# Tiny products taken away ahead of six 448-token slots, and six long warming products instead of eleven short ones

## The chip, the cores and the metric

The kernel runs on one core of one Trainium2 chip. A core has five engines with queues of their own: TensorE (PE: its products are PE, its weight loads PEld, and they overlap), VectorE (DVE), ScalarE (ACT), GpSimd (POOL) and SyncE (SP, which here issues DMAs). The metric is the device time of one execution in microseconds (us). A profile of one execution shows the span from its first to its last instruction; the execution's own time is a little longer than its span.

## The reference

Attention with a sigmoid in place of a softmax, then a mixture of experts that sends each token to one expert:

```
attention   q, k, v: (8, 12, 448, 64)
  attn = sigmoid(q k^T / 8 - log 448);  x = attn v, as (3584 tokens, 768)
experts     w1: (8, 768, 1024), w2: (8, 1024, 768)
  e(token)  = argmax(x @ w_gate);  p = its softmax probability
  g(token)  = sigmoid(x @ w_output_gate)[e]
  out       = p * g * (relu(x @ w1[e]) @ w2[e])
```

All is float32. How many tokens each expert gets is known only at run time.

## The kernel before

**Attention.** TensorE computes scores and values of all heads, 64 columns of weights at a time (lines 720 and 729). Between the stages of a batch the gate products (line 781) and the routing put each token's row into the list of its expert.

**Warming.** At the very start TensorE has no data. `attention` lets it multiply eleven times a constant column that is broadcast to 256 columns (line 811), before the first scores (line 720), which wait for the first DMAs of q and k.

**Experts, in slots.** The tokens of an expert are worked off in slots of 448 tokens, and what is left over in slots of 240 at the end. A 448-token slot does layer 1 (eight blocks f, six inner steps d each) and layer 2 (six blocks c, eight inner steps f each). Numbers are split into a high and a low part, so that each inner step is three products. In the first slot they have 448 columns each (lines 471 to 473 and 512 to 514). In every later 448-token slot the method `products` does a step with 512, 384 and 448 columns (lines 483, 484 and 485), so that layer 1 is 48 such triples and layer 2 another 48. With the inputs here seven 448-token slots run: the first from `build` with its first block begun inside the attention, three more in straight code after it (second to fourth in all), and the fifth, sixth and seventh each in a block that is entered under a condition (`tc.If`, line 936). Two 240-token slots end the kernel.

**Order of the work.** It is written out by hand (`manual_schedule`): in every block of layer 1 and layer 2 the gathers of the next slot's tokens (POOL, line 390), its weight loads (SP), and the splits of weights and tokens (ACT line 415, DVE line 416) stand between the products, so that the next slot's operands are ready when its first block comes.

**Tiny products.** `slots_begun` counts the 448-token slots that are finished. In `layer1_mm`, ahead of the first block (f == 0) of a 448-token slot, TensorE multiplies a zero tile (bfloat16) by a few of its own columns, into the PSUM bank that the block's first real product then overwrites:

```
KICKS = ((), (), (8,), (8, 8, 8), (64,), (64, 64), (128,))        # line 51
for cols in KICKS[self.slots_begun] if ... else ():               # line 465
    nc.tensor.matmul(ps[:, 0:cols], self.zero, self.zero[:, 0:cols], start=True, stop=True)
```

So there are none ahead of the first and the second slot, one of 8 columns ahead of the third, three of 8 ahead of the fourth, one of 64, two of 64 and one of 128 ahead of the fifth, sixth and seventh. Two further tiny products of the same kind (`change_step`, line 457) stand in the first slot, after its first block.

Of the kernel before, what the change touches and what calls it, by code (L numbers as in the profile page):

```python
# [30 lines left out]
TB = 448  # L31
# [16 lines left out]
ROUNDED = (12 * DF + 12 * TB) * 4  # L48
XG = GB_ * Q4 * 4
PLAIN = 6 * DF * 4 + XG + 6 * TB * 4  # L50
KICKS = ((), (), (8,), (8, 8, 8), (64,), (64, 64), (128,))


def r32(ap):
    return ap.bitcast(F32)


class Kernel:
# [400 lines left out]
    def layer1_mm(self, f, n):  # L459
        nc = self.nc  # L460
        ps = self.h_ps = self.take("h", self.psh)
        c = slice(128 * f, 128 * f + 128)
        (wh, wl), (xh, xl) = self.w1s, self.xs
        if f == 0 and n == TB:
            for cols in KICKS[self.slots_begun] if self.slots_begun < len(KICKS) else ():
                nc.tensor.matmul(ps[:, 0:cols], self.zero, self.zero[:, 0:cols], start=True, stop=True)
        for d in range(6):
            if n == TB and self.joined:
                mm = self.products(ps, wh[d][:, c], wl[d][:, c], self.x2[:, d], d == 0, d == 5)
            else:  # L470
                nc.tensor.matmul(ps[:, 0:n], wh[d][:, c], xh[:, d, 0:n], start=(d == 0), stop=False)  # L471
                nc.tensor.matmul(ps[:, 0:n], wh[d][:, c], xl[:, d, 0:n], start=False, stop=False)  # L472
                mm = nc.tensor.matmul(ps[:, 0:n], wl[d][:, c], xh[:, d, 0:n], start=False, stop=(d == 5))  # L473
            if d == 2:
                self.beat[1] = mm.ins
# [201 lines left out]
    def attention(self, pool):  # L677
        nc = self.nc
# [28 lines left out]
        def load_v(g):  # L707
            b, hp = divmod(G * g, NPAIR)
            v = vv[g % 3]
            nc.sync.dma_start(v[:, :, 0:3], self.vm[b, hp:hp + G].rearrange("g p c j d -> p g c j d"))  # L710
            for i in range(G):
                nc.sync.dma_start(v[half[i], i, 3], self.ve[b, hp + i])
# [76 lines left out]
                    want[0] = next(routes[0])  # L789

        nc.vector.memset(r32(self.rounded[:, 0:8]), 0.0)
        warm = self.rounded[:, 0:1].broadcast_to([128, 256])
        nc.vector.memset(self.bias_s, -math.log(S))
        def load_first():
            first, rest = slice(0, 128), slice(128, S)
# [11 lines left out]
        for g in (1, 2):  # L807
            load_qk(g)
            load_v(g)
        for _ in range(11):  # L810
            nc.tensor.matmul(self.ps_o[1][0][:, 0:256], warm[:, 0:128], warm, start=True, stop=True)
        LAG = 2
        for u in range(U * NG + LAG):
            g, i = divmod(u, U)
# [175 lines left out]
```

## Time and profile before

| | |
|---|---|
| time, median of 3 runs | 755.86 us (755.49 to 756.57) |
| the profiled execution's own time | 756.47 us |
| its span | 754.6 us |
| mean granted TensorE clock | 0.998 of full speed |
| PE busy | 745.1 us (99%), 5589 products |
| PEld busy | 572.3 us (76%) |
| DVE, ACT, POOL busy | 447.9, 370.4, 251.5 us (59%, 49%, 33%) |

A product's shown duration reaches past the start of the next one, since products are pipelined. What a product costs TensorE is the distance from its start to the next start.

### The profile page before, as it was taken

To read this page: it belongs to the slowest core of one execution; us is meant where nothing else is said; L and a number is where in the kernel's file an instruction comes from. 1 tells how busy PE (TensorE), PEld (TensorE's weight loads), DVE (VectorE), ACT (ScalarE), POOL (GpSimd) and SP (SyncE) were. 2 spreads that over 40 slices of the span, in tenths; PEclk is the share of its full clock that TensorE was granted. 3 is DMA by queue.
4 is the path that set the end of the run, shared out by engine and by line. 5 is a ranking of instruction groups with operands and counts; after the bars stand their busy time and mean duration, and the time that the engine had idled before them with its cause. 6 is when DMAs were issued, how large, how long until landed. Compare 5 with 4: busy or idle time off the path is not lost. (4 is left out here: it accounts for less than half of the span.)

```text
span 754.6 us, 14707 instructions
## 1 busy us (share of the span) xinstructions
PE 745.1 (99%) x5589; PEld 572.3 (76%) x5589; DVE 447.9 (59%) x895; ACT 370.4 (49%) x437; POOL 251.5 (33%) x375
## 2 busy tenths in 40 slices
PE   9999999999999999999999999999999999999996
PEld 6666444444465479999988888889989998889996
DVE  1343853586687759825836826836645665566555
ACT  6665666576776733414523514504514433444644
POOL 5000130031444436147335225315325234233461
PEclk9999999999999999999999999999999999999999
DMA  9464665746695646457387376376385476567851
GB/s 310 138 187 154 189 148 172 216 120 183 229 317 181 166 135 214 122 148 229 124 272 252 114 237 214 137 234 218 123 276 176 171 261 182 185 226 241 282 198 46
DMA packets 90647, 145.76 MB, mean 193 GB/s; under 512 B 16738, under 2 KB 67298, under 8 KB 90560
## 3 DMA queue, kind: packets, MB, share of 16 engines
q1 hardware_dynamic: 79808, 119.22, 51.1%
q0 software_dynamic: 9680, 24.53, 9.3%
q10 hardware_dynamic: 1072, 0.92, 0.5%
q8 instruction: 46, 0.75, 0.4%
q14 instruction: 41, 0.34, 0.1%
HBM read 118.40 MB, written 32.62 MB: 200 GB/s over the span
## 5 line engine op out<-in xcount | busy, mean ns | idle before, releaser
L722 ACT ACTIVATE a<-ps,small 128x896 f32<-128x896 f32 x168 | 168.9, 1007 | 84.8 <-PE ps L720 83.3
L720 PE MATMUL ps<-q,k 64*64 64x448 f32 x1344 | 179.2, 539 | 0.3
L729 PE MATMUL ps<-a,v 64*64 64x448 f32 x1344 | 178.6, 536 | 0.0
L390 POOL DMA_INDIRECT plain<-x_dram,lxs x112 | 111.0, 991 | 142.5 <-ACT h L500 66.2
L500 ACT ACTIVATE h<-ps 128x448 fp32r<-128x448 f32 (+1 forms) x72 | 36.4, 506 | 214.5 <-DVE ps L490 161.8
L729 PEld LDWEIGHTS ps<-a,v 64*64 64x64 f32 x1344 | 66.9, 133 | 62.8 <-issue 43.8
L720 PEld LDWEIGHTS ps<-q,k 64*64 64x64 f32 x1344 | 66.3, 134 | 62.8 <-issue 43.3
L483 PE MATMUL ps<-rounded 128*128 128x512 f32 x288 | 113.5, 394 | 0.0
L483 PE MATMUL ps<-h,w2h 128*128 128x512 f32 x288 | 113.1, 393 | 0.0
L485 PE MATMUL ps<-h,w2l 128*128 128x448 f32 x288 | 106.1, 368 | 0.0
L485 PE MATMUL ps<-rounded 128*128 128x448 f32 x288 | 106.0, 368 | 0.0
L416 DVE TENSOR_TENSOR rounded<-plain,rounded 128x2048 fp32r<-128x2048 f32 (+5 forms) x63 | 96.5, 1566 | 10.6 <-ACT rounded L415 10.5
L484 PE MATMUL ps<-rounded 128*128 128x384 f32 x288 | 96.8, 336 | 1.1 <-issue 1.1
L484 PE MATMUL ps<-h,w2h 128*128 128x384 f32 x288 | 96.7, 336 | 0.0
L415 ACT CAST rounded<-plain 128x2048 fp32r<-128x2048 f32 (+5 forms) x63 | 82.0, 1333 | 24.3 <-DVE plain L435 23.1
L489 DVE COPY hb<-ps 128x64 f32<-128x64 f32 x84 | 18.5, 221 | 101.2 <-PE ps L485 83.8
L575 POOL DMA_INDIRECT out<-y,lts x24 | 42.8, 1785 | 106.8 <-ACT y L568 105.0
L501 DVE SCALAR_TENSOR_TENSOR h<-ps,h 128x448 fp32r<-128x448 f32 (+1 forms) x72 | 41.3, 574 | 44.4 <-ACT h L500 37.2
L416 DVE TENSOR_TENSOR w2l<-plain,w2h 128x768 fp32r<-128x768 f32 x72 | 65.8, 954 | 3.1 <-ACT w2h L415 0.7
L485 PEld LDWEIGHTS ps<-h,w2l 128*128 128x128 f32 x288 | 54.0, 187 | 12.4
L485 PEld LDWEIGHTS ps<-rounded 128*128 128x128 f32 x288 | 54.0, 187 | 12.3
L484 PEld LDWEIGHTS ps<-rounded 128*128 128x128 f32 x288 | 54.1, 188 | 6.5 <-issue 1.5
(172 smaller groups left out, 1016.2 us busy)
## 6 DMA issues: line engine op xcount, KB each, us to landing
plain<-w SPq DMA_DIRECT2D x40, 768.0 KB
plain<-w SPq DMA_DIRECT2D x27, 1024.0 KB
k<-kT SPq DMA_DIRECT2D x23, 448.0 KB
q<-qT SPq DMA_DIRECT2D x23, 448.0 KB
x_dram<-xt SPq DMA_DIRECT2D x30, 336.0 KB
v<-vm SPq DMA_DIRECT2D x23, 384.0 KB
y<-y_dram SPq DMA_DIRECT2D x18, 384.0 KB
y_dram<-plain SPq DMA_DIRECT2D x28, 192.0 KB
```

Source lines behind the costliest of these rows:

```text
L390: self.paced(self.nc.gpsimd.indirect_dma_start(out=self.xg[:, g], out_offset=None, in_=x4, in_offset=bass.IndirectOffsetOnAxis(ap=s["lx"][ ...
L415: self.nc.scalar.copy(hi, raw)
L416: self.nc.vector.tensor_tensor(lo, raw, r32(hi), ALU.subtract)
L483: mm(ps, wh, both[:, 0:512], start=first, stop=False)
L484: mm(ps[:, 512 - TB:TB], wh, both[:, 512:2 * TB], start=False, stop=False)
L485: return mm(ps[:, 0:TB], wl, both[:, 0:TB], start=False, stop=last)
L500: self.beat[0] = nc.scalar.activation(hh, ps, AF.Relu).ins
L501: nc.vector.scalar_tensor_tensor(hl, ps, 0.0, r32(hh), ALU.max, ALU.subtract)
L575: i = self.nc.gpsimd.indirect_dma_start(out=self.out, out_offset=bass.IndirectOffsetOnAxis(ap=at, axis=0), in_=y, in_offset=None, bounds_c ...
L720: qk = nc.tensor.matmul(ps[half[h], j, 0:S], k[half[j], e, o:o + 64], q[half[j], e], start=True, stop=True)
L722: self.beat[0] = nc.scalar.activation(at[u % 3], ps[:, :, 0:S], AF.Sigmoid, bias=self.bias_s, scale=1.0 / math.sqrt(D)).ins
L729: nc.tensor.matmul(self.ps_o[e][h][half[j], 0:S], v[half[h], e, c, j], a[half[h], j], start=(i in ((0, 3 if h else 4)[e],)), stop=(i == (2 ...
```

## The change

Two edits. The table of tiny products and the loop that issues them go: no tiny product stands ahead of any 448-token slot any more (those of `change_step` in the first slot stay). And the warming products at the start are six of 512 columns instead of eleven of 256, into the same PSUM bank.

```
-KICKS = ((), (), (8,), (8, 8, 8), (64,), (64, 64), (128,))
...
     def layer1_mm(self, f, n):
...
-        if f == 0 and n == TB:
-            for cols in KICKS[self.slots_begun] if self.slots_begun < len(KICKS) else ():
-                nc.tensor.matmul(ps[:, 0:cols], self.zero, self.zero[:, 0:cols], start=True, stop=True)
         for d in range(6):
...
-        warm = self.rounded[:, 0:1].broadcast_to([128, 256])
+        warm = self.rounded[:, 0:1].broadcast_to([128, 512])
...
-        for _ in range(11):
-            nc.tensor.matmul(self.ps_o[1][0][:, 0:256], warm[:, 0:128], warm, start=True, stop=True)
+        for _ in range(6):
+            nc.tensor.matmul(self.ps_o[1][0], warm[:, 0:128], warm, start=True, stop=True)
```

## Rows read from the trace of the kernel before

**Rows 1.** The page: the span, and busy time, share and products of PE.
```profile
span 754.6 us, 14707 instructions
PE 745.1 (99%) x5589; PEld 572.3 (76%) x5589; DVE 447.9 (59%) x895; ACT 370.4 (49%) x437; POOL 251.5 (33%) x375
```

**Rows 2.** Waits of PE: line, waited for, us in total, times, longest.
```profile
PE ps L484 <- issue: 1.1, 1, 1.1
...
PE ps L471 <- DVE hb L489: 0.6, 1, 0.6
```

**Rows 3.** Windows, line 483 alone, slots two to seven: window, its us, busy (products).
```profile
329.39:385.79 56.40, 36.59 (x94) 17.46 (x93) 1.00 0.62 193
386.53:445.43 58.90, 37.65 (x95) 17.68 (x94) 1.00 0.64 213
446.21:505.10 58.89, 37.64 (x95) 17.70 (x94) 1.00 0.61 201
505.83:562.84 57.01, 36.98 (x95) 17.65 (x94) 1.00 0.64 206
566.17:621.98 55.81, 36.20 (x93) 17.27 (x92) 1.00 0.61 200
622.71:680.99 58.28, 37.25 (x95) 17.69 (x94) 1.00 0.63 205
```

**Rows 4.** Line 483, second slot: ns min/median/max, first and last start.
```profile
L483 PE MATMUL ps<-h,w2h x48: 389/389/390, 357.0 to 385.2; 128*128 128x512 f32 x48
L483 PE MATMUL ps<-rounded x46: 388/389/390, 329.4 to 356.4; 128*128 128x512 f32 x46
```

**Rows 5.** The same of the third slot.
```profile
L483 PE MATMUL ps<-h,w2h x48: 395/396/397, 415.7 to 444.8; 128*128 128x512 f32 x48
L483 PE MATMUL ps<-rounded x47: 395/396/397, 386.5 to 415.1; 128*128 128x512 f32 x47
```

**Rows 6.** Timeline of PE, second slot into third: start us, us, line.
```profile
385.58 0.37 PE L485 MATMUL ps<-h,w2l 128*128 128x448 f32 x1
385.79 0.18 PE L466 MATMUL ps<-zero 128*128 128x8 bf16 x1
385.83 0.48 PE L483 MATMUL ps<-rounded 128*128 128x512 f32 x1
...
386.53 0.40 PE L483 MATMUL ps<-rounded 128*128 128x512 f32 x1
```

**Rows 7.** Timeline of PEld there.
```profile
385.42 0.19 PEld L485 LDWEIGHTS ps<-h,w2l 128*128 128x128 f32 x1
385.79 0.10 PEld L466 LDWEIGHTS <-zero 128*128 128x128 bf16 x1 [0.18 <-issue]
```

**Rows 8.** Timeline of PE, first slot into second.
```profile
328.15 0.39 PE L483 MATMUL ps<-rounded 128*128 128x512 f32 x1
...
328.78 0.40 PE L483 MATMUL ps<-rounded 128*128 128x512 f32 x1
```

**Rows 9.** Timeline of PE, early in the sixth slot.
```profile
563.60 0.40 PE L483 MATMUL ps<-rounded 128*128 128x512 f32 x1
565.08 0.45 PE L484 MATMUL ps<-rounded 128*128 128x384 f32 x1 [1.08 <-issue]
```

**Rows 10.** Windows, all engines, fourth and fifth slot: us, busy of PE, PEld, DVE, ACT, POOL.
```profile
446.21:505.10 58.89, 58.89 (x286) 52.19 (x285) 34.55 (x59) 21.96 (x26) 20.71 (x18) 1.00 0.61 201
505.83:562.84 57.01, 57.01 (x286) 51.74 (x285) 34.32 (x59) 21.97 (x26) 20.73 (x18) 1.00 0.64 206
```

**Rows 11.** Lines 811 and 720, the start: ns min/median/max, first and last start.
```profile
L811 PE MATMUL ps<-rounded x11: 420/421/582, 0.9 to 3.2; 128*128 128x256 f32 x11
L720 PE MATMUL ps<-q,k x4: 975/1002/1003, 3.8 to 3.8; 64*64 64x448 f32 x4
L720 PE MATMUL ps<-q,k x20: 536/537/611, 4.5 to 6.2; 64*64 64x448 f32 x20
```

**Rows 12.** Timeline of PEld at the first scores.
```profile
3.75 0.33 PEld L720 LDWEIGHTS ps<-q,k 64*64 64x64 f32 x8 [0.39 <-DMA q<-qT]
```

## The prediction

> **What bounds the kernel now.** I read the page first: PE is busy 99% of the span and no other engine over 76% [rows 1]. Next the waits of PE, to see whether a data wait hides in that: after the start there are two, 1.1 us put down to issue and 0.6 us for DVE ahead of the first 240-token slot [rows 2]. So the time of the experts is the time that TensorE takes from one product to the next, and whatever shortens that distance shortens the kernel.
>
> Then I asked what one triple (512, 384 and 448 columns) takes. In windows that begin at one start of line 483, the window divided by the triples in it is the pace. Second slot: 56.40 / 94 = 0.600 us. Third: 58.90 / 95 = 0.620. Fourth: 58.89 / 95 = 0.620. Fifth: 57.01 / 95 = 0.600. Sixth: 55.81 / 93 = 0.600. Seventh, whose window ends just behind the start of its last triple: 58.28 / 94 = 0.620 [rows 3]. The same instructions thus run at two paces, 20 ns a triple apart, and nothing lies between them. Within a slot the pace does not waver: line 483 shows 388 to 390 ns in both layers of the second slot [rows 4] and 395 to 397 in both layers of the third [rows 5]. It passes from layer 1 to layer 2, with another pair of operands and another PSUM bank, unchanged. The slow pace has no cause among the data: PE waits for nothing there [rows 2], and the fourth slot (slow) and the fifth (fast) carry the same work on the other engines, DVE 59 instructions and 34.6 against 34.3 us, ACT 26 and 22.0, POOL 18 and 20.7 [rows 10].
>
> Last I looked where the pace changes. From the second slot into the third it is 0.600 before the tiny product of 8 columns and 0.620 behind it [rows 3, 6]. Three of 8 columns lie between slow and slow, one of 64 between slow and fast, two of 64 between fast and fast, one of 128 between fast and slow [rows 3]. The only slot entered without a tiny product, the second, starts with a triple of 0.63 (328.15 to 328.78), then one of 0.61, then settles at 0.600 [rows 3, 8]. I conclude that the pace is a state of the stream of products, kept while the stream runs undisturbed and thrown anew by a disturbance, and that the tiny products are such disturbances.
>
> **The change part by part.**
>
> *The tiny products themselves.* The first steady start behind each is where a window of rows 3 begins, and the window before ends at the first tiny product: 385.79 to 386.53 is 0.74, 445.43 to 446.21 0.78, 505.10 to 505.83 0.73, 562.84 to 563.60 0.76, 621.98 to 622.71 0.73 [rows 3]. Each stretch holds one real triple, worth 0.60. What is left is 0.14 + 0.18 + 0.13 + 0.16 + 0.13 = 0.74 us, all on PE's path, with nothing beside it. It goes whole, since PE waits for no data at these places and the products that follow are there already.
>
> How little of that is the product itself can be seen at the third slot: the tiny product starts at 385.79 and the real one at 385.83, but the second triple starts 0.70 later [rows 6]. The tiny product's load begins only at 385.79, 0.37 behind the load before it, with 0.18 of PEld idle [rows 7]; the loads lose their lead and the first triple pays. The Trainium skill ("TensorE: Matmul & The Clock Gate", section "Step-by-step: what each phase is for") says that PE pulls loads of weights ahead of products under way; by that a tiny product would cost no more than its own 0.04, eight of them at most 0.32, and the sum below would be some 0.4 us smaller. The load at 385.79 is not pulled ahead, so the rows decide.
>
> *The pace behind them.* If the stream keeps its 0.600 from the second slot on, three slots get faster: the third by 58.90 - 95 x 0.600 = 1.90, the fourth by 58.89 - 95 x 0.600 = 1.89, the seventh by 58.28 - 94 x 0.600 = 1.88 [rows 3]: 5.67 us. The slots that are fast now stay so. Can the other engines follow? The fifth and sixth slots do the same work as the fourth at the fast pace without a data wait [rows 2, 10], so cover is at hand; if it were gone, PE would show waits at lines 483 to 485 that name ACT or DVE. Bounds: the best is this 5.67. The worst is that the second slot falls into the slow pace and nothing throws it out: then the second, fifth and sixth lose 94, 95 and 93 times 0.020 = 5.64 [rows 3]. I take the best end: steadiness through a change of layer is shown in six slots, and a change of slot is the same kind of step, with the operands as ready.
>
> *The stall in the sixth slot.* From 563.60 to 566.17 TensorE gets through two triples [rows 3, 9], 2.57 us where the fast pace takes 1.20: 1.37 lost between 563.60 and 565.08, put down to issue. That slot begins in a block under a condition, as the fifth and seventh do, which show none [rows 2]. Taking instructions out ahead of it moves where the instructions lie, and I cannot tell from the trace whether the stall goes, stays or appears elsewhere: -1.37 to +2.7 (two more of its size). I take 0, as it is now.
>
> *Warming.* Eleven products start from 0.9 to 3.2, 0.23 apart with the slower first one [rows 11]; 256 columns at 1.2 GHz are 0.21. Six of 512 are 3072 columns in place of 2816, so the warming ends about 0.21 later. The first scores' loads come at 3.75, after 0.39 us of waiting for the DMA of q [rows 12]; that wait hides the 0.21. So 0. If the cover were gone it costs 0.21 at most. The other question is when the clock rises: score products show about 1.00 us at 3.8 and 0.54 from about 5.0 on [rows 11]. The new products fill more of the time before 3.75, which gives no reason for a later rise. Bounds: a rise before 3.8 would gain at most 0.6 (half of the 1.2 us between); one later by as much as it takes now from the first product, 0.9 to 5.0, would cost half of 4.1, 2.0. I take 0, the nearest to the rows.
>
> *Sum.* 0.74 + 5.67 = 6.41. The 240-token slots follow PE directly (their start waits 0.6 for DVE, whose work hangs on the last slot's products [rows 2]), so the gain reaches the end. The profiled execution, 756.47 with a span of 754.6, would come to 750.06. It lies 0.61 above the median of the three runs; against the median, 755.86 - 6.41 = 749.45.
>
> **The rivals.**
>
> *The slow pace from the start (slower).* The second slot is entered from the first one's products of 448 columns, and which pace it settles into may hang on a few nanoseconds. If it settles at 0.620, no tiny product throws the stream back. Place: 328. Price: 5.64 - 0.74 = +4.90, so 760.8. If the stall in the sixth slot still resets it, as the triples behind it are fast now, the second and fifth lose 3.78 and the seventh gains 1.88: +1.16, 757.0. It turns slower once more than three of the six slots are slow. For it: the settling at 328 is a matter of two triples [rows 8]. Against: it settles fast now, and what leads there keeps its order and its tiny products in the first slot. Chance 0.18 for both together, with a late clock rise or new stalls that eat the gain.
>
> *A boundary throws the pace anyway.* The fifth to seventh slots stand behind conditions; a stall at one of them may set the pace anew. One or two of the three slow slots are then won and the third stays: 0.74 + 1.89 or 0.74 + 3.78, so 753.2 or 751.3. For it: the stall of rows 9. Against: the entries to the fifth and seventh show no idle time. Chance 0.19.
>
> *The pace is not the tiny products' doing.* The slots have the paces they have for some other reason, and only 0.74 goes: 755.1. [...] That the change doesn't reach the pace, or wins one slot and loses another, has 0.11.
>
> **How the numbers follow.** The forecast has 0.52, own range 748.0 to 751.5: with the stall gone 749.45 - 1.37 = 748.1, with one more 750.8, and the 0.6 by which runs of one kernel differ. The second rival (0.19) is faster too. About 0.2%, 1.5 us, is what a measurement can tell from no change. Faster: 0.52 + 0.19 = 0.71; same 0.11; slower 0.18. The range must take in the second and third rival and the small end of the first: 748.0 to 757.0, which leaves out the fully slow case and a gain beyond the forecast.
>
> **What would show it.** Right: windows of line 483 give 0.600 in all six later slots; from line 485 of one slot to line 483 of the next 0.20 us and no row of line 466; first scores at 3.8. Wrong: 0.620 in a slot, which names the rival by which slot it is; a wait of PE on ACT or DVE in the third, fourth or seventh slot; idle time put down to issue at another entry; score products still at 1.00 us behind 5.0.

## The result and the profile after

The changed kernel takes 748.71 us (median of 4 runs, 748.18 to 749.37) against 756.00 for the one before (755.49 to 756.57): a ratio of 0.9896, 95% interval 0.9881 to 0.9911. The profiled execution took 749.12. Line numbers from 467 on are 4 lower than before: 479 to 481 are the triple, 467 to 469 the products of 240 columns, 716 and 725 scores and values, 807 the warming.

The page of the changed kernel, span and PE:

```profile
span 747.3 us, 14681 instructions
...
PE 739.1 (99%) x5576; PEld 544.7 (73%) x5576; DVE 447.2 (60%) x895; ACT 369.8 (49%) x437; POOL 250.4 (34%) x375
```

PE is still the bound [rows 1]. Its waits (line, waited for, us in total, times, longest):

```profile
PE ps L807 <- DVE small L789: 0.9, 1, 0.9
PE ps L467 <- DVE hb L485: 0.6, 1, 0.6
PE ps L777 <- issue: 0.2, 1, 0.2
```

The 1.1 us put down to issue in a triple [rows 2] is gone, and no data wait has come in its place.

The windows of line 479 in the second to seventh slot (window, its us, PE busy and products, PEld busy and loads, clock, DMA), which answer to [rows 3]:

```profile
329.81:386.21 56.40, 36.57 (x94) 17.65 (x94) 1.00 0.63 192
386.21:443.81 57.60, 37.34 (x96) 18.02 (x96) 1.00 0.65 218
443.81:501.41 57.60, 37.34 (x96) 18.02 (x96) 1.00 0.63 208
501.41:559.01 57.60, 37.34 (x96) 18.02 (x96) 1.00 0.64 210
559.01:616.61 57.60, 37.34 (x96) 18.02 (x96) 1.00 0.62 206
616.61:673.63 57.02, 36.98 (x96) 17.84 (x95) 1.00 0.61 200
```

A product that reaches over an edge is counted too, so a count can be one more than the triples that a window spans. Each of the middle four is one whole slot: 57.60 / 96 = 0.600 us a triple. The last window ends just behind the start of its last triple, so 57.00 / 95 = 0.600 too. All six slots run at the fast pace, and the windows follow each other without a gap. The timeline of PE at the boundary of the second and third slot shows why, against [rows 6]:

```profile
386.01 0.36 PE L481 MATMUL ps<-h,w2l 128*128 128x448 f32 x1
386.21 0.39 PE L479 MATMUL ps<-rounded 128*128 128x512 f32 x1
...
386.81 0.39 PE L479 MATMUL ps<-rounded 128*128 128x512 f32 x1
```

0.20 from slot to slot and 0.60 to the next triple: TensorE does not notice the boundary.

The start did move. The timeline of PE, first the changed kernel, then the one before:

```profile
0.94 2.93 PE L807 MATMUL ps<-rounded 128*128 128x512 f32 x6 [0.94 <-DVE small L789]
3.80 3.84 PE L716 MATMUL ps<-q,k 64*64 64x448 f32 x24
7.47 0.93 PE L725 MATMUL ps<-a,v 64*64 64x448 f32 x8
```

```profile
3.78 2.91 PE L720 MATMUL ps<-q,k 64*64 64x448 f32 x24
6.50 0.94 PE L729 MATMUL ps<-a,v 64*64 64x448 f32 x8
```

The first scores start within 0.02 us of each other, but the first values come 0.97 later, because the scores ran at a lower clock for longer: four of them take 0.75 from 5.34 to 6.09 in the changed kernel, and 0.38 from 5.00 to 5.38 in the one before. The window view shows a granted clock of 1.00 for this stretch in both, so the level (1.2 or 2.4 GHz) is read from these distances here. At the second slot's first triple (328.58, against 328.15 in [rows 8]) the changed kernel is 0.43 behind.

### The profile page after: what moved, and what is told of

It is laid out like the page before. It is cut to its first block, busy times and chain, and to the rows that moved or that the text cites. A ratio compares the mean times of both kernels' runs of the same rounds, so it can differ in the third digit from the quotient of the medians.

```text
span 747.3 us, 14681 instructions
## 1 busy us (share of the span) xinstructions
PE 739.1 (99%) x5576; PEld 544.7 (73%) x5576; DVE 447.2 (60%) x895; ACT 369.8 (49%) x437; POOL 250.4 (34%) x375
## 5 line engine op out<-in xcount | busy, mean ns | idle before, releaser
L716 PE MATMUL ps<-q,k 64*64 64x448 f32 x1344 | 157.6, 542 | 0.0
L725 PE MATMUL ps<-a,v 64*64 64x448 f32 x1344 | 155.9, 536 | 0.0
L479 PE MATMUL ps<-rounded 128*128 128x512 f32 x288 | 112.0, 389 | 0.0
L716 PEld LDWEIGHTS ps<-q,k 64*64 64x64 f32 x1344 | 50.5, 134 | 76.5 <-issue 69.8
L725 PEld LDWEIGHTS ps<-a,v 64*64 64x64 f32 x1344 | 51.0, 133 | 75.4 <-issue 71.4
L481 PEld LDWEIGHTS ps<-rounded 128*128 128x128 f32 x288 | 54.1, 188 | 11.1
L254 POOL TENSOR_TENSOR meta<-eom,den 64x1 f32<-64x1 f32 (+1 forms) x40 | 8.0, 199 | 152.2 <-DVE eom L251 150.5
```

The costliest lines, as they stand in the source:

```text
L479: mm(ps, wh, both[:, 0:512], start=first, stop=False)
L481: return mm(ps[:, 0:TB], wl, both[:, 0:TB], start=False, stop=last)
L716: qk = nc.tensor.matmul(ps[half[h], j, 0:S], k[half[j], e, o:o + 64], q[half[j], e], start=True, stop=True)
L725: nc.tensor.matmul(self.ps_o[e][h][half[j], 0:S], v[half[h], e, c, j], a[half[h], j], start=(i in ((0, 3 if h else 4)[e],)), stop=(i == (2 ...
```

## The experiments

**The tiny products out, the old warming kept.**

```
 the changed kernel, with
-        for _ in range(6):   ... 512 columns
+        for _ in range(11):  ... 256 columns
```

> The tiny products are out, the eleven warming products of 256 columns stay. Theory (pace is a state that a tiny product throws anew, and that a boundary between slots leaves alone): 0.600 us a triple in all six later slots, no row of the tiny products, and 6.4 to 7.8 us less than before (the 1.4 between them is the stall in the sixth slot), so 748.2 to 749.6. Rival (the warming decides on the pace, by the time at which the scores start): some of the third, fourth and seventh slots stay at 0.620, over 750.

749.56 us (748.02 to 752.19), ratio 0.9915 (0.9882 to 0.9947). The profiled execution took 748.02 and has 0.600 in all six slots; two of its windows of line 479:

```profile
385.21:442.81 57.60, 37.34 (x96) 18.02 (x96) 1.00 0.66 222
...
558.01:615.61 57.60, 37.34 (x96) 18.02 (x96) 1.00 0.62 204
```

The first edit makes the gain, and in this profile the warming does not decide on the pace. Two of the four times (752.19 and 750.42) lie where the rival had them, over 750, so the kernel ran again:

> The same kernel as in the first of these runs (tiny products out, eleven warming products of 256 columns), whose four times spread from 748.0 to 752.2. If in some executions the pace is thrown in the last one or two slots, the times stand in groups about 1.9 us apart (748, 750, 752); if it was the chip, they lie within 1.5 us as those of the changed kernel did (748.2 to 749.4).

747.87 us (747.26 to 748.89), ratio 0.9889 (0.9869 to 0.9908), within 1.7 us; its profile has 0.600 throughout. The two high times did not come back, and no profile shows what made them. The kernel before, run beside the first of these, spread as far (755.43 to 759.18). That stays open.

**The new warming alone.**

```
 the kernel before, with
-        for _ in range(11):  ... 256 columns
+        for _ in range(6):   ... 512 columns
```

> Six warming products of 512 columns, the tiny products as before. Theory: paces 0.600, 0.620, 0.620, 0.600, 0.600, 0.620 in the second to seventh slot as before, time within 1.0 us of before (756.0), the start up to 0.5 later since the clock rose later in the profile of the changed kernel. If the stall in the sixth slot hangs on where the instructions lie, five products fewer ahead of it may take up to 1.4 away. Rival (the warming made the gain): 750 or less.

755.35 us (754.87 to 756.00), ratio 0.9984 (0.9973 to 0.9994). The paces are those of before; two windows of line 483, third and fifth slot (58.90 / 95 = 0.620, 57.01 / 95 = 0.600):

```profile
386.77:445.67 58.90, 37.62 (x95) 17.67 (x94) 1.00 0.64 214
...
506.07:563.08 57.01, 36.95 (x95) 17.64 (x94) 1.00 0.64 207
```

The median is 0.97 us lower; between the two profiles, 0.75 lies in the sixth slot's stall. In the timeline of PE it now stands here:

```profile
563.84 0.40 PE L483 MATMUL ps<-rounded 128*128 128x512 f32 x1
...
564.46 0.40 PE L483 MATMUL ps<-rounded 128*128 128x512 f32 x1
...
564.87 0.37 PE L485 MATMUL ps<-rounded 128*128 128x448 f32 x1
565.56 0.50 PE L483 MATMUL ps<-rounded 128*128 128x512 f32 x1 [0.33 <-issue]
```

That is behind the ninth real product of the slot; before it was behind the fourth [rows 9]. Five warming products fewer ahead, five products later. From 564.46 to 566.28 two triples take 1.82 in place of 1.20, so it costs 0.62 in place of 1.37. The lines show one thing more: between the two tiny products of 64 columns and the stall, a triple takes 0.62 (563.84 to 564.46), and behind the stall the pace is 0.600. So the pair seems to have led from fast to slow here, and the stall back to fast; in the kernel before, line 483 shows 0.40 at the same place [rows 9], as in its slow slots.

**One tiny product in the whole kernel's later slots.** Two kernels, with one tiny product ahead of the third slot, of 8 columns in the first and 64 in the second:

```
 the changed kernel, with the loop of line 465 and
+KICKS = ((), (), (8,))          # the other: (64,)
```

> The changed kernel with one tiny product of 8 columns ahead of the third slot and none elsewhere. Theory: the third slot goes to 0.620 and, since nothing throws the pace again, so do the fourth to seventh: 0.14 + 5 x 96 x 0.020 = 9.7 us over the changed kernel, about 758.4, slower than before although four of five slots have fewer tiny products. Rival (a tiny product disturbs only the slot that it precedes, the paces belong to the slots): third slot alone slow, +2.1, about 750.8.

> The changed kernel with one tiny product of 64 columns ahead of the third slot and none elsewhere. In the kernel before, 64 columns took the stream from 0.620 to 0.600. Theory A (the shape of the disturbance decides on the pace behind it): 0.600 throughout, 0.14 over the changed kernel, 748.9. Theory B (a tiny product swaps one pace for the other): 0.620 from the third slot on, +9.7, about 758.4. Rival (paces belong to the slots): 0.600 except at most one slot, under 751.

758.29 us (757.62 to 759.31), ratio 1.0019 (1.0007 to 1.0031) with 8 columns; 757.91 (757.39 to 759.18), ratio 1.0022 (1.0010 to 1.0033) with 64. Both are slower than the kernel before. Windows of line 483 with 8 columns, second to seventh slot:

```profile
328.71:385.12 56.41, 36.57 (x94) 17.45 (x93) 1.00 0.62 192
385.86:444.76 58.90, 37.62 (x95) 17.86 (x95) 1.00 0.63 207
444.76:504.28 59.52, 38.02 (x96) 18.05 (x96) 1.00 0.63 206
504.28:563.80 59.52, 38.02 (x96) 18.05 (x96) 1.00 0.62 199
563.80:623.32 59.52, 38.02 (x96) 18.05 (x96) 1.00 0.62 198
623.32:682.24 58.92, 37.64 (x96) 17.86 (x95) 1.00 0.63 203
```

0.600 before the tiny product, 59.52 / 96 = 0.620 in every slot behind it, through four boundaries. One tiny product costs 5 x 96 x 0.020 = 9.6 us of pace. The rival by which paces belong to slots falls: the fifth and sixth slots, fast before, are slow here. Two windows with 64 columns, third and fourth slot:

```profile
386.13:445.03 58.90, 37.62 (x95) 17.86 (x95) 1.00 0.64 214
445.03:504.55 59.52, 38.02 (x96) 18.05 (x96) 1.00 0.61 199
```

In the kernel before, 64 columns led from slow to fast [rows 3]; here, from fast, they lead to slow. So the length of the tiny product does not choose the pace (theory A falls): a single one swaps it. All of them bring the same load of a 128x128 bf16 tile (of `zero`) with them; no run varies it, so it is not shown whether the product or its load does this.

**What one and two tiny products do to either pace.**

```
 the changed kernel, with the loop of line 465 and
+KICKS = ((), (), (8,), (8,), (8, 8), (128,), (64, 64))
```

> The changed kernel with tiny products of 8, 8, twice 8, 128 and twice 64 columns ahead of the third to seventh slot: to see what each does to either pace. Theory B (each tiny product swaps the pace): 0.620 in the third, 0.600 in the fourth, 0.600 in the fifth, 0.620 in the sixth and 0.620 in the seventh. Theory A' (8 always leads to 0.620): 0.620 in the fourth too. One look; its time follows from the paces, 748.7 + 0.7 + 1.92 for every slow slot (755.2 for three).

754.64 us, one execution. Windows of line 483, second to seventh slot:

```profile
328.89:385.30 56.41, 36.57 (x94) 17.46 (x94) 1.00 0.63 191
386.04:444.94 58.90, 37.62 (x95) 17.67 (x95) 1.00 0.63 212
445.67:502.68 57.01, 36.95 (x95) 17.65 (x94) 1.00 0.63 206
504.04:562.32 58.28, 37.22 (x94) 17.48 (x93) 1.00 0.63 204
563.05:620.06 57.01, 36.96 (x95) 17.65 (x94) 1.00 0.63 208
620.82:679.12 58.30, 37.25 (x95) 17.67 (x94) 1.00 0.62 201
```

Fast, then 8: slow (0.620); 8: fast (57.01 / 95 = 0.600); 8 and 8: slow (58.28 / 94 = 0.620); 128: fast; 64 and 64: slow. Each single one swapped, as theory B has it; with [rows 3] and the two kernels above, 8, 64 and 128 columns have now been seen to swap both ways. Two in a row did not swap twice: my expectation for them was wrong both times. Both pairs led from fast to slow, as the pair in the kernel with the new warming alone seems to have done; what a pair does to the slow pace was not seen. The three of 8 columns in the kernel before left the slow pace slow [rows 3]. What several in a row do stays without a rule.

**As many products ahead of the sixth slot as before, none of them ahead of a later slot.**

```
-                self.change_step()       # in the first slot, after its first block
+                self.change_step(14)
```

> The changed kernel with 12 more tiny products of 8 columns in the first slot (14 in place of 2 after its first block), so that as many products stand ahead of the sixth slot as in the kernel before; none ahead of later slots. In the kernel before the stall of 1.37 us comes behind the fourth real product of the sixth slot; with the tiny products in and five warming products fewer it came about 0.9 us later in the slot and cost 0.6; in the changed kernel it is gone. Theory (the stall hangs on where the instructions of the sixth slot lie): it is back at the fourth product, about 1.4 us, and the pace behind it is thrown anew: 0.600 or 0.620 for the sixth and seventh slot. Time 748.7 + 0.4 + 1.4 = 750.5, or 754.3 if the two last slots turn slow. Rival (the tiny products just ahead of the sixth slot made the stall): no stall, 749.1.

757.60 us (755.45 to 760.60), ratio 1.0025 (1.0006 to 1.0043), far over both expectations. Windows of line 479, second, third, fifth, sixth and seventh slot:

```profile
327.51:386.41 58.90, 37.62 (x95) 17.86 (x95) 1.00 0.62 191
386.41:445.93 59.52, 38.02 (x96) 18.05 (x96) 1.00 0.63 210
...
505.45:564.97 59.52, 38.02 (x96) 18.05 (x96) 1.00 0.62 199
566.58:622.98 56.40, 36.57 (x95) 17.64 (x94) 1.00 0.63 210
622.98:680.00 57.02, 36.98 (x96) 17.83 (x95) 1.00 0.62 201
```

Two things happened. The second slot settled at 0.620 and nothing took it out until the sixth: the prediction's first rival, brought about by twelve tiny products a whole slot ahead. And the stall is back, at the fourth product as expected, in the timeline of PE:

```profile
565.59 0.40 PE L479 MATMUL ps<-rounded 128*128 128x512 f32 x1
566.10 0.44 PE L480 MATMUL ps<-rounded 128*128 128x384 f32 x1
```

So its place goes with how many products stand ahead, not with tiny ones just before. Its size does not: 0.99 us for a triple of 0.62, 0.37 lost, where I expected 1.4. It threw the pace from 0.620 to 0.600, so the two last slots, 56.40 / 94 and 57.0 / 95, are fast. The ten times stand in two groups, 755.5 to 756.1 and 759.1 to 760.6. One more execution was profiled:

> The kernel with 14 tiny products in the first slot once more, for one more profile. Its ten times stood in two groups, five of 755.5 to 756.1 and five of 759.1 to 760.6; the profile was of the first, with the stall in the sixth slot throwing the pace from 0.620 to 0.600. Theory: in the second group the stall leaves 0.620 behind it, 2 x 96 x 0.020 = 3.84 us for the sixth and seventh slot; if this execution is of that group, its profile has 0.620 in all six. Rival (the groups are of the chip or the start): paces as in the first profile at a time of 759 to 760.

757.12 us, and again the stall behind the fourth product (0.24 lost) took 0.620 to 0.600. Its time lies between the two groups. The second group was not caught in a profile; that the stall leaves the slow pace there is a guess that fits the 3.8 us and no more.

**Other triples.** Does the pace belong to the three lengths and their order? First another order, then other lengths with the same 1344 columns and the same sums (448 is written for `TB`, and the `start` and `stop` flags are left out; with 480 the column counts in `join` change too):

```
 512, 448, 384 (in place of 512, 384, 448)
-  mm(ps[:, 64:448], wh, both[:, 512:896])
   mm(ps[:, 0:448], wl, both[:, 0:448])
+  mm(ps[:, 64:448], wh, both[:, 512:896])
```

```
 480, 416, 448
-  mm(ps, wh, both[:, 0:512])
-  mm(ps[:, 64:448], wh, both[:, 512:896])
+  mm(ps[:, 0:480], wh, both[:, 0:480])
+  mm(ps[:, 32:448], wh, both[:, 480:896])
   mm(ps[:, 0:448], wl, both[:, 0:448])
```

> The changed kernel with the last two products of a triple swapped: 512, 448, 384 columns instead of 512, 384, 448; the sums are the same, in another order. If the two paces belong to the order of the three lengths, this shows other ones, steady again. 576 triples: 10 ns a triple are 5.8 us. Theory: another pair of paces, so a time of 748.7 plus or minus 6 to 12; rival (the pace goes by the columns alone, 1344 a triple): 0.600 and 748.7.

> The changed kernel with triples of 480, 416 and 448 columns in place of 512, 384 and 448; the same 1344 columns and the same sums. 1344 columns at 2.4 GHz are 560 ns, and the lengths in place now give 600 or 620. Theory (the pace belongs to the lengths and their order): another pace, in a steady state; if under 0.600, it beats the changed kernel by 5.8 us per 10 ns. Rival: 0.600 again, 748.7.

The other order: 754.16 us (753.72 to 755.08), ratio 0.9979 (0.9966 to 0.9992). Its triples do not settle. Line 479 in the third and fourth slot (ns min/median/max) varies by 10 ns, where [rows 4, 5] vary by 2, and the fifth slot with one triple on either side takes 59.35 / 97 = 0.612:

```profile
L479 PE MATMUL ps<-rounded x95: 393/397/403, 386.2 to 473.1; 128*128 128x512 f32 x95
```

```profile
502.45:561.80 59.35, 38.52 (x97) 18.20 (x98) 1.00 0.63 200
```

480, 416 and 448: 749.76 us (749.64 to 749.85), ratio 0.9916 (0.9891 to 0.9941), steady at 57.93 / 96 = 0.603 in the fourth slot:

```profile
443.44:501.37 57.93, 36.20 (x97) 17.99 (x96) 1.00 0.63 208
```

The pace does go with the lengths and their order. Neither variant is under 0.600; no version here beats the changed kernel.

**No warming at all, and the changed kernel beside it.**

```
-        for _ in range(6):
-            nc.tensor.matmul(self.ps_o[1][0], warm[:, 0:128], warm, start=True, stop=True)
```

> The changed kernel without any warming product: the doubled dose of the second edit. The profiles so far have the clock rise between 3.8 and 6.9 us, earlier or later under either warming, and each us of it costs half a us. Theory (the warming pays, which of the two forms it has does not matter): the clock rises some 3 us later than with warming, 1.5 us more than the changed kernel run beside it. Rival (it does nothing): within 0.5 us of it. The paces stay at 0.600 if they don't hang on the start.

> The changed kernel once more, beside the one without warming and on the same chip; 748.2 to 749.4, all six later slots at 0.600, no stall. Its ratio to the kernel before, against 0.9889 for the tiny products out under the old warming, says what the new warming is worth: nothing (0.988 to 0.991) by theory, 0.985 or 0.993 if it is worth 3 us one way or the other.

Without warming 748.43 us (748.06 to 749.61), ratio 0.9904 (0.9878 to 0.9930); the changed kernel on the same chip 747.36 (746.99 to 747.99), ratio 0.9884 (0.9859 to 0.9910). No time of the one overlaps one of the other, so warming seems worth about 1.1 us; with four times of each that is not much evidence, since the changed kernel's own median was 748.71 in the first series and 747.36 in this one. Its form is worth nothing that shows: 0.9915 and 0.9889 with eleven, 0.9896 and 0.9884 with six. The timeline of PE without warming:

```profile
3.74 3.99 PE L716 MATMUL ps<-q,k 64*64 64x448 f32 x24 [3.74 <-DMA k<-kT]
7.55 0.94 PE L725 MATMUL ps<-a,v 64*64 64x448 f32 x8
```

First values at 7.55, hardly behind the 7.47 and 7.36 of the two profiles of the changed kernel, so the profiles do not show where the 1.1 us lie.

## Why the prediction was right

749.45 was forecast, 748.71 measured. Between the two profiled executions the span shrank by 7.3 us. From the second slot's first triple to the seventh slot's last it shrank from 680.99 - 328.15 = 352.84 to 673.61 - 328.58 = 345.03, by 7.81; the stretch ahead of it gave back 0.43 and the tail (73.61 before, 73.69 after) 0.08. The 0.43 is no cost of the change that the runs show: in the other profile of the changed kernel the second slot starts at 327.36, earlier than the 328.15 before.

**The tiny products themselves and the pace, 0.74 + 5.67.** Right, and shown: all six slots at 0.600, boundaries of 0.20. Taking the tiny products out under the old warming brings the gain, and the new warming alone does not. That the pace is kept across a boundary was argued from the change of layer; one tiny product ahead of the third slot shows it through four boundaries, at the slow pace.

**What throws it.** "Thrown anew" was too loose. A single tiny product of 8, 64 or 128 columns swaps the pace. That is why the kernel before alternated: one of 8 lost the pace, one of 64 got it back, one of 128 lost it again [rows 3]. The prediction read the two of 64 as standing between fast and fast; the kernel with the new warming alone suggests that they led to slow and that the stall, four products later, led back.

**The stall, taken at 0 within -1.37 to +2.7.** It went: 7.81 is 0.74 + 5.67 + 1.37 and 0.03 of rounding. The kernels with five products fewer and with the count of before restored show that its place follows the number of products ahead, one for one. Why it is gone with seven fewer (the old warming) or twelve (the changed kernel) is not shown; with five fewer it came later and was smaller. Nor is it shown what it waits for: one instruction transfer of 0.02 MB falls between 562 and 563 us in the kernel before, but the changed kernel has one between 558 and 559, also at the entry of the sixth slot, and no stall. The term was taken at 0 "as it is now" and was worth 1.37, the larger part of what the forecast missed. That the miss is only 0.74 is partly luck, since the 0.43 and the 0.08 went the other way.

**Warming, taken at 0.** Right for the form. The wait for q did hide the longer warming (first scores at 3.80 against 3.78). But the time at which the clock rises could not be had from one profile: the 24 first scores took from 2.49 to 4.00 in the ten profiles with six warming products (3.84 and 3.68 in the two of the changed kernel), from 2.81 to 3.17 in the three with eleven, and 3.99 in the one without. So the 0.97 between the two kernels' first profiles is no mark of the new warming. The Trainium skill ("TensorE: Matmul & The Clock Gate", section "What's actually happening") says that the number of products that run at the lower clock differs between runs of one kernel; these profiles agree.

**The rivals.** The slow pace from the second slot on did not come, but it is real: twelve more tiny products in the first slot brought it, at 757.60. That a boundary throws the pace is shown only where the sixth slot has its stall. That the pace is not the tiny products' doing falls: one put in or taken out decides on it.

## What to carry to other kernels

When TensorE is the bound and waits for nothing, compute the distance from one group of products to the next group of the same kind, stretch by stretch: busy shares hide a 3% difference that two windows show. If the same instructions have two paces, look at the rows where it changes, and test a suspected disturbance by putting in a single one: if it is a state, the effect lasts far beyond the place. Filler products chosen for one version of a kernel belong to that version; twelve of them in another slot changed the pace of the four slots that followed.

## What was not expected of the hardware

Two steady paces were seen for the triple in the order 512, 384, 448 (0.600 and 0.620) and one of 0.603 with 480, 416, 448; with 512, 448, 384 the triples vary about 0.612. A single product of 8, 64 or 128 columns swaps the two. The Trainium skill ("TensorE: Matmul & The Clock Gate", section "Back-to-back issue gap") gives N / 2.4 + 2.5 ns at the full clock for a product by itself; summed for the three lengths, an estimate, that is 567.5 ns. It adds that in a stream of weight loads and products both set the distance; no stream of these triples here came under 600 ns. A stall of PE moved by five products when five were taken out far ahead of it, and cost between 0.24 and 1.37 us in four profiles.
